# One load of V's weights becomes two, in a fused attention and gated-MLP kernel

## The chip, the cores and the metric

The kernel runs on one core of a Trainium2 chip. The metric is the device time of one execution in microseconds (us). It was measured three times for the kernel before: median 308.36, from 307.97 to 308.63.

## The reference

The input x has 2048 rows of 640 numbers (bf16). The rows are normalized, and two branches of the result are added to x: sliding-window attention with 32 heads of 20 columns and a window of 256 rows, and a gated MLP of width 1536.

```python
xn = _layernorm(x)
q, k, v = split(xn @ wqkv)                  # wqkv is 640 x 1920: Q, K and V columns
p = softmax(where(mask, q @ k.T * 20**-0.5, -1e9))   # causal, 256 back
A = (p @ v) @ wo
B = (sigmoid(xn @ w_gate) * (xn @ w_up)) @ w_down
return x + A + B
```

## The kernel before

The 2048 rows are worked in four chunks of 512, a chunk in four blocks of 128 rows. Every product contracts over 640 numbers, so it takes five matmuls that add into one accumulator, one for each contraction block of 128. For that the normalized rows have to be transposed: `xnT[0][:, d, ...]` holds contraction block d of chunk 0. The order on every engine is that in which the code is written; each engine runs its own list in order and waits on semaphores where it needs the work of another.

The change touches the start, chunk 0. It goes like this.

**Loads.** SP issues the loads one after the other (L183 to L190): the rows of blocks 0, 1 and 3 of x (`load_rows`, L177, 160 KB each), the weights of V's columns 0 to 319 (`load_v(0)`, L181, 400 KB: 128 partitions, five contraction blocks, 320 columns of two bytes), the rows of block 2, V's columns 320 to 639 (`load_v(1)`), and Q's and K's weights (`load_wqkv`, L171, 800 KB each). Later come parts of the gate and up weights (L202) and zeros for two scratch tensors (L199). All go into one queue that 16 DMA engines serve; each engine moves its share of every transfer and reports its end, and a transfer has landed at the sixteenth report. Eight semaphores are handed out to the transfers in turn, so from the ninth on a transfer is issued only when the one eight places before it has landed.

**Normalizing.** For blocks 0 and 3, DVE makes mean and variance (L268, L274) and ACT the root (L654). For blocks 1 and 2, ACT makes the mean (`mean_act`, L664), the sum of squares (L669) and the root (L670). DVE then takes a reciprocal (L658 or L674) and writes the normalized rows `xn` (L292 or L675).

**Transposing.** PE transposes five 128x128 pieces of a block into `pt` (`transpose_rows`, L299), and ACT (block 0, in pieces of three and two) or DVE (the others) copies them to `xnT` (L300).

**V.** `project_v(c, s, hf)` (L364 to L371) multiplies block s with the weights of column half hf: five matmuls over 320 columns (L368) into a PSUM tile of the pool `ps_d`, which has four buffers handed out in turn. `copy_v` (L377) then casts the result into the V tiles, 64 rows per instruction, on DVE or ACT.

These steps are interleaved by hand between L679 and L716. On PE the order is: transposes of block 0; seven warming matmuls; transposes of block 1; V of block 0, first half (v00 in the code); v10; transposes of block 3; v01; v30; v11; transposes of block 2; v31; and both halves of block 2. After that come Q and K of chunk 0 (`g_qk`, L331), then the MLP and attention, with PE at work almost without a break. The first `ps_d` buffer goes to the warming matmuls, the next to v00, v10 and v01; v30 takes the warming buffer again, v11 that of v00, v31 that of v10. A buffer can be written again when its casts are done. The casts of v00 are one on DVE and one on ACT:

```python
    xn2, neg2 = mean_act(2)
    r2 = root_act(2, xn2, neg2)
    norm(3, mv3, r3)
    v10 = project_v(0, 1, 0)
    copy_v(0, 0, 0, v00, dve, (0,))
    transpose_rows(3, dve)
    v01 = project_v(0, 0, 1)
    norm_act(2, xn2, neg2, r2)
    copy_v(0, 0, 0, v00, act, (1,))
```

Of the kernel before, what the change touches and what calls it, by code (L numbers as in the profile page):

```python
# [15 lines left out]
DC = D // P  # L16
# [9 lines left out]
HALF = 320  # L26
# [86 lines left out]
def kernel(  # L113
# [11 lines left out]
    nc = tc.nc  # L125
# [36 lines left out]
    wv = const.tile([P, DC, D], BF16, name="wv")  # L162
    wqkv_r = A_wqkv.rearrange("(c p) n -> p c n", p=P)
# [12 lines left out]
    def load_rows(s, queue):  # L176
        queue.dma_start(out=xc[0][:, s, :], in_=xr[:, s, :])  # L177

    def load_v(hf):
        a = 2 * D + hf * HALF  # L180
        nc.sync.dma_start(out=wv[:, :, hf * HALF:(hf + 1) * HALF], in_=wqkv_r[:, :, a:a + HALF])  # L181

    load_rows(0, nc.sync)  # L183
    load_rows(1, nc.sync)
    load_rows(3, nc.sync)
    load_v(0)
    load_rows(2, nc.sync)
    load_v(1)
    load_wqkv(0)
    load_wqkv(1)  # L190
# [662 lines left out]
```

## Time and profile before

The profiled execution took 308.43 us; its span, from the first to the last instruction, is 306.7.

| | us | share of the span |
|---|---|---|
| PE (matmuls) | 299.9 | 98% |
| ACT | 197.5 | 64% |
| DVE | 179.9 | 59% |
| POOL | 173.0 | 56% |
| 0 to 2 us: PE busy, DMA share | 1.16 | 0.09 |
| 2 to 14 us: PE busy, DMA share | 11.41 of 12.00 | 1.01 |
| 14 us to the end: PE busy, DMA share | 287.30 of 292.70 | 0.36 |

A busy PE includes warming matmuls, which compute nothing of the result; up to 5.3 us PE does nothing else. The DMA share is the mean busy share of the 16 DMA engines. The views used below are the chain of work that ended last (followed back from the last instruction), the timeline of the engines' instructions with the idle time before each and what released it, the sums of a stretch, and the trace's completion events of each transfer. L-numbers are lines of the kernel. The granted clock of PE is 1.00 in every stretch.

### The profile page before, as it was taken

What the parts mean: (1) busy time and instruction counts of PE and PEld (TensorE: products, weight loads), DVE (VectorE), ACT (ScalarE), POOL (GpSimd) and SP (SyncE); (2) the same over time, 40 slices, a digit from 0 to 9 for tenths busy, and PEclk for the clock granted to TensorE, in tenths of its full rate; (3) what the DMA queues carried; (4) which work ended last, traced back from release to release, by engine and by line L of the source; (5) the groups of instructions that cost most, each with busy time, mean ns of one, the idle gap of its engine ahead of it and who ended that gap; (6) DMA issues with size and microseconds to landing.
All of it is one profiled execution on the core that took longest, in us unless ns stands there. A gap on an engine that the chain in (4) does not pass through costs nothing.

```text
span 306.7 us, 10106 instructions
## 1 busy us (share of the span) xinstructions
PE 299.9 (98%) x4341; PEld 168.0 (55%) x4376; DVE 179.9 (59%) x356; ACT 197.5 (64%) x194; POOL 173.0 (56%) x314
## 2 busy tenths in 40 slices
PE   8999999999999999999999999999999999999996
PEld 6654444445657654554557654554546664444774
DVE  5735657889866569683826555482733527362433
ACT  6833768688965648888655538979585557778000
POOL 3086667479873728676572827657372756557000
DMA  7998959646574152773001222650000210000202
GB/s 209 364 316 253 320 185 260 206 129 194 141 231 111 44 161 83 235 221 75 4 0 47 65 70 80 193 177 2 2 2 2 66 45 25 0 4 0 88 24 64
DMA packets 40148, 36.04 MB, mean 118 GB/s; under 512 B 9000, under 2 KB 39848, under 8 KB 40104
## 3 DMA queue, kind: packets, MB, share of 16 engines
q1 hardware_dynamic: 39240, 34.63, 37.1%
q10 hardware_dynamic: 864, 0.77, 0.8%
q8 instruction: 34, 0.56, 0.8%
q14 instruction: 10, 0.08, 0.1%
HBM read 24.77 MB, written 10.62 MB: 115 GB/s over the span
## 4 chain that ended last, share of the span: by engine, by line
PE 96%; DMA 2%; issue 1%; SPq 0%; DVE 0%
PE y L481 18%; PE pu L467 17%; PE pg L460 17%; PE pqk L331 14%; PE ps L536 9%; PE pv L368 8%; PE y L488 7%; PE acc L567 6%; DMA wv<-in_A_wqkv_dram 2%; SPq L177 0%; PE pt L299 0%; DVE xn L492 0%
## 5 line engine op out<-in xcount | busy, mean ns | idle before, releaser
L548 POOL TENSOR_SCALAR_AFFINE_SELECT pT<-pT 64x512 bf16<-64x512 bf16 (+1 forms) x252 | 152.4, 605 | 90.7 <-ACT pT L541 79.0
L541 ACT ACTIVATE pT<-ps 128x2048 bf16<-128x2048 f32 x75 | 140.8, 1877 | 58.8 <-PE ps L536 57.8
L471 DVE SCALAR_TENSOR_TENSOR h<-th,pu 128x512 bf16<-128x512 f32 x48 | 32.7, 683 | 55.9 <-PE pu L467 42.7
L467 PE MATMUL pu<-xnT,wu 128*128 128x512 bf16 x230 | 58.9, 380 | 0.7 <-issue 0.3
L460 PE MATMUL pg<-xnT,wg 128*128 128x512 bf16 x225 | 58.3, 380 | 1.2 <-issue 0.6
L481 PE MATMUL y<-wd,h 128*128 128x320 bf16 (+2 forms) x396 | 56.6, 295 | 0.0
L331 PE MATMUL pqk<-xnT,wqk 128*128 128x512 bf16 x190 | 44.9, 380 | 0.7 <-issue 0.3
L481 PEld LDWEIGHTS <-h 128*128 128x128 bf16 x396 | 36.7, 98 | 15.9 <-issue 2.2
L463 ACT ACTIVATE th<-pg 128x512 f32<-128x512 f32 x48 | 28.6, 596 | 15.3 <-PE pg L460 15.1
L460 PEld LDWEIGHTS <-wg 128*128 128x128 bf16 x240 | 22.2, 98 | 25.7 <-issue 2.0
L467 PEld LDWEIGHTS <-wu 128*128 128x128 bf16 x240 | 22.1, 98 | 25.4 <-issue 1.8
L536 PE MATMUL ps<-qT,kT 20*64 20x320 bf16 (+4 forms) x1456 | 31.9, 259 | 0.0
L331 PEld LDWEIGHTS <-wqk 128*128 128x128 bf16 x200 | 19.5, 103 | 21.2 <-issue 1.2
L579 DVE STREAM_TRANSPOSE t<-acc 128x512 f32<-128x512 f32 x32 | 21.1, 695 | 13.7 <-PE acc L567 13.7
L536 PEld LDWEIGHTS <-kT 20*64 20x64 bf16 x1456 | 15.7, 103 | 24.5 <-issue 22.0
L492 DVE SCALAR_TENSOR_TENSOR rows<-y,rows 128x320 bf16<-128x320 f32 x30 | 14.3, 484 | 21.4 <-PE y L488 21.1
L368 PE MATMUL pv<-wv,xnT 128*128 128x320 bf16 x160 | 25.8, 300 | 0.3 <-DMA wv<-in_A_wqkv_dram 0.3
L488 PE MATMUL y<-wo,oc 128*128 128x320 bf16 (+2 forms) x165 | 24.2, 295 | 0.0
L567 PE MATMUL acc<-pT,v 64*32 64x320 bf16 (+4 forms) x1456 | 19.7, 252 | 0.0
L567 PEld LDWEIGHTS <-v 64*32 64x32 bf16 x1456 | 16.4, 91 | 5.9 <-ACT pT L541 1.3
L368 PEld LDWEIGHTS <-xnT 128*128 128x128 bf16 x160 | 14.6, 98 | 8.9 <-issue 1.6
L591 DVE TENSOR_TENSOR on<-t,rec 128x320 bf16<-128x320 f32 (+1 forms) x32 | 18.6, 580 | 1.1
(52 smaller groups left out, 187.8 us busy)
## 6 DMA issues: line engine op xcount, KB each, us to landing
qT<-sq SPq DMA_DIRECT2D x16, 256.0 KB
kT<-sk SPq DMA_DIRECT2D x16, 256.0 KB
sq<-st SPq DMA_DIRECT2D x20, 128.0 KB
sk<-st SPq DMA_DIRECT2D x20, 128.0 KB
out_dram<-rows SPq DMA_DIRECT2D x15, 160.0 KB
wg<-in_B_w_gate_dram SPq DMA_DIRECT2D x4, 480.0 KB
wu<-in_B_w_up_dram SPq DMA_DIRECT2D x4, 480.0 KB
xc<-in_A_x_dram SPq DMA_DIRECT2D x3, 640.0 KB
```

Of the source, the lines that this page charges most:

```text
L331: nc.tensor.matmul(ps, lhsT=wt[:, m, :], rhs=xnT[c][:, d, :], start=(d == 0), stop=(d == DC - 1))
L368: nc.tensor.matmul(ps[:, 0:HALF], lhsT=xnT[c][:, d, s * P:(s + 1) * P], rhs=wv[:, d, hf * HALF:(hf + 1) * HALF], start=(d == 0), stop=(d = ...
L460: nc.tensor.matmul(pg, lhsT=part(wg, d, f), rhs=xnT[c][:, d, :], start=(d == 0), stop=(d == DC - 1))
L463: nc.scalar.activation(out=th, in_=pg, func=TANH, scale=0.5)
L467: nc.tensor.matmul(pu, lhsT=part(wu, d, f), rhs=xnT[c][:, d, :], start=(d == 0), stop=(d == DC - 1))
L471: nc.vector.scalar_tensor_tensor(out=h, in0=th, scalar=1.0, in1=pu, op0=ADD, op1=MULT)
L481: nc.tensor.matmul(y[:, 0:cut[1] - cut[0]], lhsT=ht[c, f][:, s * P:(s + 1) * P], rhs=wd[:, f, cut[0]:cut[1]], start=(f == 0), stop=False)
L488: nc.tensor.matmul(y[:, 0:cut[1] - cut[0]], lhsT=oc[c, m][:, s * P:(s + 1) * P], rhs=wo[:, m, cut[0]:cut[1]], start=False, stop=(m == DC - 1))
L536: nc.tensor.matmul(ps[a * U:(a + 1) * U, i, col * U:(col + n) * U], lhsT=qk["k", kc, o // GH][32 * i:32 * i + DH, o % GH + a, kb * U:(kb + ...
L541: nc.scalar.activation(out=pt[:, :, 0:CW], in_=ps, func=EXP, scale=SCALE)
L548: nc.gpsimd.affine_select(out=view, in_=view, pattern=[[0, HG], [0, n], [sign, U]], compare_op=GE, fill=0.0, base=base, channel_multiplier ...
L567: nc.tensor.matmul(acc[32 * i:32 * i + 32, q * U:(q + n) * U], lhsT=vt[kb][a * U:(a + 1) * U, u, h * VW:h * VW + 32], rhs=pt[a * U:(a + 1) ...
```

## The change

`load_v` gets a range of contraction blocks, and the first column half is loaded by two transfers in a row: blocks 0 to 2 (240 KB) and blocks 3 to 4 (160 KB). Every other load keeps its place behind them, and the second column half stays one transfer.

```diff
-    def load_v(hf):
+    def load_v(hf, lo=0, hi=DC):
         a = 2 * D + hf * HALF
-        nc.sync.dma_start(out=wv[:, :, hf * HALF:(hf + 1) * HALF], in_=wqkv_r[:, :, a:a + HALF])
+        nc.sync.dma_start(out=wv[:, lo:hi, hf * HALF:(hf + 1) * HALF], in_=wqkv_r[:, lo:hi, a:a + HALF])
 
     load_rows(0, nc.sync)
     load_rows(1, nc.sync)
     load_rows(3, nc.sync)
-    load_v(0)
+    load_v(0, 0, 3)
+    load_v(0, 3, DC)
     load_rows(2, nc.sync)
     load_v(1)
     load_wqkv(0)
```

In the instruction lists, SP has one transfer more, and the fourth matmul of v00 waits for the second of the two. K's weights become the ninth transfer, which waits for the landing of block 0's rows. All other instructions, their order and what they wait for are the same; after the first transfers the semaphores are handed out one place further on.

## The prediction

> **What bounds the kernel now.** I read the page first, then the chain of work that ended last from 0 to 34 us, then the timeline of each engine from 6 to 14 us, and last the sums of that stretch.
>
> ```profile
> PE 299.9 (98%) x4341; PEld 168.0 (55%) x4376; DVE 179.9 (59%) x356; ACT 197.5 (64%) x194; POOL 173.0 (56%) x314
> ```
>
> PE is busy 98% of the 306.7 us span, and the later chain is almost all PE. So whatever the start gains or loses is carried to the end one for one, and nothing else is in play. The chain in the start (start us, us, what):
>
> ```profile
> 2.19 4.92 DMA wv<-in_A_wqkv_dram
> 7.11 0.04 issue
> 7.15 1.52 PE pv L368 x10
> 8.67 0.28 PE pt L299 x5
> 8.95 2.12 PE pv L368 x15
> 11.06 0.28 PE pt L299 x5
> 11.34 2.15 PE pv L368 x15
> ```
>
> It says that the first half of V's weights lands at 7.11 and that PE runs from there. Taken alone, this promises the whole wait to the change. But the chain names one releaser per step and hides those that came a few hundredths earlier. They are in the timeline (start, us, engine, line, idle before):
>
> ```profile
> 6.68 0.10 PEld L368 LDWEIGHTS <-xnT 128*128 128x128 bf16 x1
> ...
> 7.15 1.52 PE L368 MATMUL pv<-wv,xnT 128*128 128x320 bf16 x10 [0.25 <-DMA wv<-in_A_wqkv_dram]
> ...
> 7.56 0.74 ACT L664 ACTIVATE xn<-xc 128x640 bf16<-128x640 bf16 x1 [0.20 <-DMA xc<-in_A_x_dram]
> ...
> 9.70 2.19 ACT L377 CAST v<-pv 64x320 bf16<-64x320 f32 x5
> 9.70 0.16 DVE L674 RECIPROCAL rstd<-rstd 128x1 f32<-128x1 f32 x1 [0.23 <-ACT rstd L670]
> 9.90 0.45 DVE L675 TENSOR_SCALAR xn<-xc,neg,rstd 128x640 bf16<-128x640 bf16 x1
> 10.38 1.00 DVE L377 CAST v<-pv 64x320 bf16<-64x320 f32 x2
> ...
> 11.41 0.49 DVE L300 COPY xnT<-pt 128x640 bf16<-128x640 bf16 x1
> ...
> 11.95 1.20 PEld L368 LDWEIGHTS <-xnT 128*128 128x128 bf16 x10 [0.27 <-DVE xnT L300]
> ```
>
> The second chain to see: rows of block 2 (xc) land just before 7.56. From there ACT (mean, squares, root; its rows at 8.42 and 9.38 are among those left out), then DVE (reciprocal, normalize, two casts of v01, copy of the transpose) run without a free moment up to 11.90, and PE's last two V products start on that copy at 11.95.
>
> **The change, step by step.** I write vst for the product of row block s with column half t; PE's order is v00, v10, transposes of block 3, v01, v30, v11, transposes of block 2, v31, v20, v21. A V matmul starts every 0.135 us ((1.52-0.30)/9, 0.30 being the length of one), so a product of five takes 0.68; a transpose takes 0.056 (0.28/5).
>
> *Removed: the wait for blocks 3 and 4.* The weights' load for v00 starts at 6.68; a later product starts its first matmul 0.05 after its load (8.73 and 8.78), so v00 could start at 6.73. It starts at 7.15: 0.42 us wait. The second part is 128x2x640 = 163,840 bytes, at the 328 GB/s of 4.6 to 6.8 us 0.50 us of transfer. So my estimate for the first part is 7.11-0.50 = 6.61, ahead of the 6.69 that no wait needs. Bounds: 7.11 (all of the wait stays) and 6.73 or earlier (all goes).
>
> *Added: a wait on v00's fourth matmul* for blocks 3 and 4. Queued behind it on PE is everything else. It comes at 6.73+3x0.135 = 7.14; the data at about 7.11. Cost 0.00 to 0.04, and the next step covers it.
>
> *What is late next.* v10 needs xnT of block 1: DVE copies it 6.95 to 7.43, so 7.49 instead of 7.82 (0.33 left). Transposes of block 3 after it: 8.17 (their input is ready at 8.04). v01 could start at 8.45, but needs the second column half, whose last completion event in the trace is at 8.64: 8.68 instead of 8.78 (0.10 left). v30 starts when v01's matmuls are through, 9.36, instead of 9.53. v11 writes the accumulator of v00, which ACT reads in the first of the casts from 9.70, 0.42 each: 10.12, plus 0.05 to PE, 10.17 instead of 10.22 (0.05 left). v20 needs the copy of block 2 at 11.41 to 11.90: 11.95, as now. **0.00 left.** From v20 to the Q projection at 13.32 PE is dense, and it stays so.
>
> So the wait of 0.42 is cut into pieces and stands again ahead of v10, v01, v11 and v20. The start is worth what block 2's landing moves, and nothing else.
>
> *Moved: block 2's rows, V's second half and Q's and K's weights are issued one SP instruction later*, 0.48 us (2.19 to 2.67). In the queue this does not show if the 16 engines are behind anyway. DMA share 1.01 and 1.07 from 4.6 us on (sums of the stretches, next-to-last column) and this row of SP say they are:
>
> ```profile
> 3.71 2.26 SPq L171 DMA_DIRECT2D wqk<-in_A_wqkv_dram  x2
> ```
>
> An issue takes 0.43 to 0.53 when free; two take 2.26 here, because SP is held up by a full queue. Block 2 is issued at 2.67 and used at 7.56; block 0 is issued at 0.80 and used at 3.11. Thus some 2.6 us of the 4.89 are queueing, and 0.48 hides in them. The cost of a further transfer in the queue itself is not to be seen in before alone. From above, 0.48 (the issue pitch, as if nothing hid it). From below, -0.59: PE's idle places from 6.73 to 13.32 sum to 0.42+0.07+0.10, and block 2 can't give more than PE can take. Block 2's 163,840 bytes follow the half of wv within 0.45 (7.11 to 7.56), which at 363 GB/s are their own transfer time: a boundary between transfers costs nothing there. That is the nearest row, and I take 0.00. Q's weights are used 13.19 and K's near 18.7 (13.32+25x0.216, the first 25 matmuls of Q and K at five to 1.08); the completion events have them at 10.91 and 13.20, so 0.48 is covered there.
>
> *Waits on eight-back transfers.* Each transfer from the ninth on waits for the one eight before it; one more transfer makes K's weights the ninth, waiting for block 0 (used 3.11, issue after 4.28): 0. All other waits keep their partners from there on, and compute instructions and their order are the same but for the one wait.
>
> Sum: 308.43 (the profiled execution: 306.7 span and 1.73 around it; the median is 308.36, the runs 307.97 to 308.63) + 0.00 = **308.4**.
>
> The Trainium skill speaks for splitting under a condition: "Perfetto Trace Analysis", section DMA Optimizations, says that smaller pieces may start sooner if the DMA engines are generally idle. The shares above say that this condition is not met, and by that rule the sum would be the same.
>
> **The rivals.**
>
> *A. Slower: block 2 lands later.* The DMA share dips to 0.73 (151 GB/s) from 3.4 to 4.6, when the engines turn from x to V's weights, and the sixteenth completion of that transfer comes at 7.11, the fifteenth at 6.41. One engine pays 0.70 for its start. If the second transfer makes it pay again, block 2, v20 and the end come 0.70 later: 309.1; with only the issue slip, 308.9. It decides as soon as the landing comes after 7.56, for there is no slack behind. For it: the dip. Against it: no such lag is added at block 2 or wv's second half, which follow in a full queue.
>
> *B. Faster: the dip fills.* Smaller pieces let engines that now wait start sooner, and block 2 lands earlier. Half of what PE can take, 0.3, gives 308.1; the limit 0.59 gives 307.8. For: the same dip. Against: bytes and packets are the same, and the late engine has its first packets in the first part either way.
>
> *C. It does not do what it says:* the late engine holds back the first part too, to 7.1. PE waits as now: 308.4. The fifteen others landed by 6.41, so all hangs on that engine.
>
> *D. A fixed price per transfer, in series.* A lone transfer takes 2.31 (0.80 to 3.11) from issue to use; if block 2 had to wait for that once more: 310.7. Against: the 0.45 above. The Trainium skill, "DMA: Bandwidth & Descriptors", section Anatomy of one DMA, gives about 2.0 us fixed per transfer (for those issued by GpSimd); by that 310.4; the trace's 0.45 between two landings speaks against paying it in series.
>
> **How the numbers follow.** 0.2% is 0.62 us, about what a measurement of this kernel can tell from no change. Forecast 0.50, C 0.12, B 0.13, A 0.22, D 0.03. Forecast and C stay within 0.62 but for the runs' own scatter of about 0.3 (0.02 faster, 0.04 slower). B reaches 0.62 only at its limit with scatter: 0.08 of 0.13 faster. A passes it at 0.70: 0.16 of 0.22 slower; D all. So faster 0.10, same 0.67, slower 0.23. The range: from B's limit less a little scatter, 307.7, to A's 309.1 with a little, 309.2.
>
> **What would show it.** After: v00 starts near 6.73; PE's idle time for wv is gone or 0.04; ACT's first pass over block 2 still starts at 7.5 to 7.6; v20's load waits longer for DVE's copy (0.27 now); the Q projection starts at 13.3. If it starts earlier, block 2 landed earlier (B); later with a late ACT pass, A. I am wrong in the working if the Q projection moves while ACT's pass does not, or if the end moves while the Q projection doesn't.

## The result and the profile after

The changed kernel takes 309.2 us (median of 11 runs, 308.61 to 309.68); the kernel before took 308.36 beside it (11 runs, 307.97 to 308.83). The ratio is 1.0026, with a 95% interval of 1.0018 to 1.0034: slower by 0.8 us. The profiled execution of after took 309.34, with a span of 307.5 (308.43 and 306.7 before).

The page of after:

```profile
span 307.5 us, 10107 instructions
...
PE 300.0 (98%) x4341; PEld 168.3 (55%) x4376; DVE 180.2 (59%) x356; ACT 197.4 (64%) x194; POOL 172.8 (56%) x314
```

PE's busy time grew by 0.1, the span by 0.8. So PE does the same work and stands idle longer. From the first matmul of the Q projection to the last of PE, the traces have 290.61 before and 290.49 after. All of the loss is ahead of the Q projection, which starts at 14.12 instead of 13.32. The chain of work that ended last, in the start (start us, us, what):

```profile
3.70 5.94 DMA wv<-in_A_wqkv_dram
9.64 0.04 issue
9.69 2.20 PE pv L369 x15
11.88 0.28 PE pt L300 x5
12.16 2.12 PE pv L369 x15
14.28 0.22 PE pqk L332
```

Before, the weights in the chain were those issued at 2.19, V's first half. Now they are those issued at 3.70: **V's second half**, a transfer that the change does not touch. The timeline shows where PE stands (start, us, engine, line, idle before):

```profile
6.78 1.60 PE L369 MATMUL pv<-wv,xnT 128*128 128x320 bf16 x10
...
7.31 0.72 ACT L665 ACTIVATE xn<-xc 128x640 bf16<-128x640 bf16 x1
...
7.52 0.52 PEld L369 LDWEIGHTS <-xnT 128*128 128x128 bf16 x5 [0.24 <-DVE xnT L301]
...
9.69 2.20 PE L369 MATMUL pv<-wv,xnT 128*128 128x320 bf16 x15 [1.03 <-DMA wv<-in_A_wqkv_dram]
...
12.75 1.20 PEld L369 LDWEIGHTS <-xnT 128*128 128x128 bf16 x10 [0.24 <-DVE xnT L301]
```

v00 starts at 6.78 instead of 7.15, v10's load waits for the copy of block 1 at 7.52, and ACT's pass over block 2 starts at 7.31 instead of 7.56. All this is early or as forecast. Then v01 stands 1.03 us for the second column half, which landed at 9.64 (8.64 before). (The listed idle counts from the modelled end of the matmul before it. By start times the wait is 1.19: in before v01 follows the first transpose of block 3 after 0.28, here after 1.47.) v00 started 0.37 earlier than before, v01 starts 0.91 later (9.69 against 8.78).

SP's rows of after (start, us):

```profile
2.18 0.96 SPq L181 DMA_DIRECT2D wv<-in_A_wqkv_dram  x2
3.19 0.47 SPq L177 DMA_DIRECT2D xc<-in_A_x_dram  x1
3.70 0.43 SPq L181 DMA_DIRECT2D wv<-in_A_wqkv_dram  x1
```

V's second half is issued at 3.70 instead of 3.23 and lands 1.00 later: the 0.47 of its place, and 0.53 more. The sums from 6 to 8 us (the last two columns are the DMA share and GB/s), of before and then of after:

```profile
6.00:8.00 2.00, 1.47 (x15) 0.96 (x13) 1.93 (x6) 1.17 (x4) 0.00 (x0) 1.00 1.06 349
```

```profile
6.00:8.00 2.00, 2.00 (x22) 1.48 (x21) 1.93 (x7) 1.54 (x5) 0.00 (x0) 1.00 0.83 214
```

The queue that the forecast took for full did not stay so in after. In the stretch in which block 2 ends and V's second half begins, its engines moved 214 GB/s instead of 349.

### The profile page after: what moved, and what is told of

The parts are those of the page before. It is cut to its first block, busy times and chain, and to the rows that moved or that the text cites. A ratio compares the mean times of both kernels' runs of the same rounds, so it can differ in the third digit from the quotient of the medians.

```text
span 307.5 us, 10107 instructions
## 1 busy us (share of the span) xinstructions
PE 300.0 (98%) x4341; PEld 168.3 (55%) x4376; DVE 180.2 (59%) x356; ACT 197.4 (64%) x194; POOL 172.8 (56%) x314
## 4 chain that ended last, share of the span: by engine, by line
PE 95%; DMA 2%; issue 1%; SPq 1%; DVE 0%
PE y L482 18%; PE pu L468 17%; PE pg L461 17%; PE pqk L332 14%; PE ps L537 9%; PE y L489 7%; PE pv L369 7%; PE acc L568 6%; DMA wv<-in_A_wqkv_dram 2%; SPq L177 1%; SPq L181 0%; DVE xn L493 0%; PE pt L300 0%
```

## The experiments

Two theories. **The place**: a further transfer ahead of V's second half makes SP issue that half 0.48 later, and its landing follows its issue; that the further transfer is a split does not matter. **The split** (the rival): the pieces themselves, their boundary or their smaller size, cost time in the engines. In the expectations theory 1 is the place, theory 2 the split, and theory 3 an accident of one execution. Ratios are against the kernel before on the same chip, with 95% intervals.

### Both kernels once more

No edit.

> The changed kernel once more, for a second trace. In its first trace V's second column half landed at 9.64 us (8.64 before) and PE waited 1.03 us for it, while block 2 landed at 7.06 (7.54 before). Theory 1 (issue slip: whatever stands one place later in SP's list comes later) and theory 2 (thin queue: with the smaller pieces the engines reach V's second half with little queued, and pay for its start again) both expect the wait again, 0.7 to 1.1 us, and a ratio near 1.0026. Theory 3 (accident of one execution, with the loss elsewhere) expects a wait that is far from 1.0, 0 to 0.4.

> The kernel before once more, one look. Theories 1 and 2 expect V's second half at 8.5 to 8.8 us and no wait of PE for it, with the wait for the first half (0.3 to 0.5) and block 2 near 7.5. Theory 3 expects one of the two to move by half a us or more.

After again: 308.93 (10 runs), ratio 1.0018 (1.0006 to 1.0031). Its profiled execution shows the same wait in the same place; V's second half, issued at 3.69, landed at 9.82:

```profile
9.86 2.20 PE L369 MATMUL pv<-wv,xnT 128*128 128x320 bf16 x15 [1.03 <-DMA wv<-in_A_wqkv_dram]
```

Before again, one run, 308.28 with a span of 306.5:

```profile
6.79 1.60 PE L368 MATMUL pv<-wv,xnT 128*128 128x320 bf16 x10
...
8.50 2.28 PE L368 MATMUL pv<-wv,xnT 128*128 128x320 bf16 x15
```

Here V's first half landed at 6.61 and v00 waited for no weights. The wait of 0.42 that the forecast set out to remove belongs to one execution of before. Of the seven traces with this half unsplit in its old place (before twice and five experiments), none of the other six has it. In one of them it is hidden by chance: with the small transfer behind V's second half the first half landed at 6.97, and v00's weights were loaded only at 6.94, since PE's earlier work came late.

The expectation for before again was missed: 8.5 to 8.8 for V's second half and the old wait. It landed at 8.13, about half a us earlier, which had been given as a sign of theory 3. The landings do scatter that much; the ratios of after in two sets of runs, 1.0026 and 1.0018, say that the loss is no accident.

### A small transfer in place of the split

```diff
     load_v(0)
+    dum = const.tile([P, 32], BF16, name="dum")
+    nc.sync.dma_start(out=dum, in_=xr[:, 2, 0:32])
     load_rows(2, nc.sync)
```

The 8 KB are not used. It was run twice, the second time on another chip.

> The kernel before with the first half of V's weights in one transfer, and a small extra transfer (128 rows of 64 bytes of x into a tile nobody reads) behind it, where the second part stands in the changed kernel. Block 2 and V's second half are so issued one place later, without the split. Theory 1: V's second half lands near 9.6, PE waits for it 0.7 to 1.0, ratio 1.002 to 1.003. Theory 2: the first half holds the engines up as before, the second half lands at 8.6 to 8.8, ratio 1.000 to 1.0006. Theory 3: ratio 1.000.

> The small extra transfer instead of the split again (the kernel before with 128 rows of 64 bytes loaded where the second part stands), in more rounds, since its first interval held both theories. Theory 1 (the later issue alone makes V's second half late): ratio 1.0018 to 1.003, and a wait of PE for V's second half of 0.7 or more. Theory 2 (the split itself, by the thinner queue, makes it late): ratio 0.9995 to 1.0008 and a wait of 0 to 0.3. A ratio between, 1.0008 to 1.0018, with a wait near the 0.36 of its first trace: each gives a part.

308.55, ratio 1.0011 (0.9994 to 1.0028, 10 runs), and 308.84, ratio 1.0019 (1.0009 to 1.0029, 11 runs). In the first trace V's second half was issued at 3.70, landed at 9.02, and PE waited; ratio and wait lie between the two theories:

```profile
9.06 2.20 PE L370 MATMUL pv<-wv,xnT 128*128 128x320 bf16 x15 [0.36 <-DMA wv<-in_A_wqkv_dram]
```

In the second trace the same half, issued at 3.69, landed at 8.61:

```profile
8.65 2.20 PE L370 MATMUL pv<-wv,xnT 128*128 128x320 bf16 x15
```

No idle time is listed, and by start times the wait is 0.19 (8.65, 0.47 after the first transpose of block 3, instead of 0.28). So the ratio is the one that theory 1 expected, the wait the one that theory 2 expected. That execution took 308.22, near the lower end of its runs: five of them lie from 308.17 to 308.49, six from 308.84 to 309.48. So a small transfer with no split costs, within the intervals, what the change costs, but not the same in each execution. One trace alone would have misled here.

### The second half ahead of block 2

After, with the two loads exchanged, so that V's second half gets its old issue time back and block 2 pays for it.

```diff
-    load_rows(2, nc.sync)
     load_v(1)
+    load_rows(2, nc.sync)
```

> The changed kernel with V's second half issued ahead of block 2, so that it is issued when it was before (near 3.2 us), and block 2 a place after it. Theory 1: V's second half lands at 8.2 to 8.7 and PE waits for it 0 to 0.2; block 2 lands at 7.5 to 8.2, and what it is late after 7.56 stands ahead of v11 or v20: ratio 1.000 to 1.002. Theory 2: V's second half still starts in a thin queue, lands at 9.0 to 9.4 and PE waits 0.4 to 0.8; ratio 1.002 to 1.004.

309.93, ratio 1.0041 (1.0023 to 1.0059, 5 runs). V's second half, issued at 3.19, landed at 7.92 and v01 did not wait for it. Block 2, issued at 3.70, landed at 8.40 (7.06 in after). ACT's pass over it started 0.99 after ACT was free, ACT's casts came later, and v11, which writes a buffer that ACT has to read first, stood for them:

```profile
8.43 0.74 ACT L665 ACTIVATE xn<-xc 128x640 bf16<-128x640 bf16 x1 [0.99 <-DMA xc<-in_A_x_dram]
```

```profile
11.04 0.84 PE L369 MATMUL pv<-wv,xnT 128*128 128x320 bf16 x5 [0.91 <-ACT v L378]
```

The ratio lies above both ranges (1.000 to 1.002 for theory 1, 1.002 to 1.004 for theory 2), and the landing at 7.92 is earlier than both. V's second half has its old issue time here, but the 160 KB of block 2 now come behind it and not ahead, so its early landing does not test the place alone. And block 2 has the 400 KB of V ahead of it: it landed 0.48 after them, about the 0.43 that it took behind the first half in before (7.11 to 7.54). Its lateness goes with its turn in the queue and can't be put down to the slot. That block 2 has little room was right.

### The split without the later place: part of the loads on ACT's queue

Three kernels take one early load off SP's list and give it to ACT, which I expected to issue it at about 2.3, behind its table load. `scr` is the tile of ACT's first small instruction, moved ahead and fed from the constants, so that it waits for nobody.

```diff
+    nc.scalar.activation(out=scr, in_=ones[:, 0:1], func=SQRT)
     load_v(0, 0, 3)
-    load_v(0, 3, DC)
+    load_v(0, 3, DC, nc.scalar)
...
-    nc.scalar.activation(out=scr, in_=eps, func=SQRT)
```

`load_v` gets the queue as a further argument. The second kernel is before with `load_rows(2, nc.scalar)` and no split; the third is after with `load_rows(2, nc.scalar)`; both have `scr` moved in the same way.

> The split without the later issue: blocks 0 to 2 from SP as in the changed kernel, blocks 3 to 4 from ACT's queue at about 2.3 us, where ACT has nothing to do (the activation that loads ACT's table reads a constant instead of eps, so that it need not wait). SP's list is then as before, block 2 at 2.7 and V's second half at 3.2. Theory 1: V's second half lands at 8.1 to 8.7, PE waits 0 to 0.2 for it; ratio 0.999 to 1.0005. Theory 2: it lands at 9.2 or later, PE waits 0.5 to 1.0; ratio 1.0015 to 1.003.

> No split; block 2's rows are issued from ACT's queue at about 2.3 us, so that V's second half moves one place up in SP's list (2.7 instead of 3.2). Theory 1: its landing follows its issue, 7.7 to 8.2, no wait; block 2 lands earlier than 7.0, so PE's waits ahead of v20 shrink; ratio 0.998 to 0.9995 if the first half is not much later than 6.7. Theory 2 says the same of block 2 and expects V's second half no earlier than 8.1; ratio 0.9985 to 1.0.

> The split as in the changed kernel, both parts from SP, with block 2's rows from ACT's queue at about 2.3 us: V's second half is issued at 3.2, as before the change. Theory 1: lands at 8.1 to 8.7, PE's wait for it 0 to 0.2, ratio 0.998 to 1.0003. Theory 2: lands at 9 or later, PE waits 0.4 to 0.9, ratio 1.001 to 1.003.

Ratios 1.0013 (1.0004 to 1.0021, 11 runs), 1.0016 (1.0007 to 1.0026, 12 runs) and 1.0013 (1.0004 to 1.0022, 11 runs). The intended issue time was missed. ACT issued at 0.86, beside its table load, and its transfer ran among the rows of x. Block 1 landed at 4.09 instead of 3.5, and ACT's first pass, the head of the chain to v00, came late. ACT's queue and first pass in the first of the three:

```profile
0.86 0.45 ACTq L181 DMA_DIRECT2D wv<-in_A_wqkv_dram  x1
...
4.11 0.74 ACT L665 ACTIVATE xn<-xc 128x640 bf16<-128x640 bf16 x1 [1.82 <-DMA xc<-in_A_x_dram]
```

PE of the same kernel:

```profile
7.29 1.60 PE L369 MATMUL pv<-wv,xnT 128*128 128x320 bf16 x10
...
9.01 2.28 PE L369 MATMUL pv<-wv,xnT 128*128 128x320 bf16 x15
```

v00 starts at 7.29 and v01 at 9.01 without a wait for weights. That is a price of its own, about 0.5, and it hides the total. All three ratios lie above the ranges of theory 1 (the first in neither range, the second above both, the third in theory 2's), but with this price in them they decide nothing between the theories. The landing can be read all the same: with the split kept and V's second half issued at 3.18 and 3.19, it landed at 7.81 and 7.93 (first and third kernel). In these two traces the boundary within the first half does not delay it. The second kernel, issued at 2.66, landed it at 8.85, which the place alone does not explain. The Trainium skill ("Perfetto Trace Analysis", section DMA Optimizations) suggests spreading DMAs over the engines that can issue them where issuing is the limit; these three ratios do not bear it out here, since the second queue delayed the rows.

### The second part on ACT's queue, issued later

The same with ACT's first instruction left in its old place (it ends at 3.0) and the load behind it.

```diff
     nc.scalar.activation(out=scr, in_=eps, func=SQRT)
+    load_v(0, 3, DC, nc.scalar)
```

> After, but the second part (blocks 3 and 4) goes through ACT's queue, issued after ACT's one early instruction (the row that waits for eps until 2.80), so at about 3.0. SP's list is then that of before: block 2 at 2.67, V's second half at 3.2. Theory of the place (V's second half is late because SP issues it one place later): second half lands at 8.7 or earlier, PE waits under 0.1 ahead of v01, v00 starts near 6.8, Q projection 13.0 to 13.35, ratio 0.998 to 1.0005. Theory of the split (one more transfer of weights costs wherever it is issued): second half lands after 9, PE waits 0.4 or more ahead of v01, Q projection 13.7 or later, ratio 1.0015 or more. A transfer in a queue of its own may also delay block 2; that would show as ACT's first pass over block 2 after 7.6.

309.94, ratio 1.0062 (1.0044 to 1.008, 6 runs): a miss of both theories. ACT issued at 3.57, not at 3.0: as the tenth transfer in turn, it was handed the semaphore of block 1's rows and waited for their landing, at 3.55. By then ACT's first pass was due, and behind the issue it moved from 3.54 to 4.11. The part landed at 8.38, and PE stood within v00:

```profile
3.57 0.49 ACTq L181 DMA_DIRECT2D wv<-in_A_wqkv_dram  x1
```

```profile
7.29 0.57 PE L369 MATMUL pv<-wv,xnT 128*128 128x320 bf16 x3
...
8.42 1.11 PE L369 MATMUL pv<-wv,xnT 128*128 128x320 bf16 x7 [0.56 <-DMA wv<-in_A_wqkv_dram]
```

It shows what the added wait on v00's fourth matmul costs when its cover is gone. It does not separate the theories, since V's second half (issued at 3.19, landed at 8.71) shared the engines with this part.

### The small transfer behind, and two of them ahead

```diff
     load_v(1)
+    dum = const.tile([P, 32], BF16, name="dum")
+    nc.sync.dma_start(out=dum, in_=xr[:, 2, 0:32])
     load_wqkv(0)
```

> Before with one small transfer (32 columns of block 2's rows, 8 KB, not used) behind V's second half instead of ahead of block 2. Q's and K's weights go one place later, V's second half keeps its place at 3.2. Theory of the place: second half lands as in before (8.1 to 8.7), no new wait, ratio 0.999 to 1.0005. Theory of the further transfer (any one more transfer in these queues costs): ratio 1.0015 or more, as with the small transfer ahead of block 2 (1.0019).

308.38, ratio 1.0007 (0.9997 to 1.0016, 12 runs). V's second half was issued at 3.21, landed at 8.51, and v01 did not wait:

```profile
8.71 2.28 PE L370 MATMUL pv<-wv,xnT 128*128 128x320 bf16 x15
```

By the trace the place decides. By the time alone it is open: 1.0007 lies between the two expectations, a little above that of the place, and its interval overlaps that of the small transfer ahead (1.0009 to 1.0029).

The second kernel has two such transfers (columns 0 to 31 and 32 to 63) behind `load_v(0)`, so V's second half comes two places later.

> Before with two small transfers (8 KB each, not used) ahead of block 2: the suspected cost twice. V's second half is issued at about 4.2 instead of 3.22, block 2 at about 3.7. Theory of the place: second half lands at 9 to 10 and PE waits 0.4 to 1.4 ahead of v01, with less scatter than with one place; ratio 1.002 to 1.005, more than the 1.0019 of one. If the cost does not grow with the places (1.001 to 1.002 again), the place is not the cause.

309.23, ratio 1.0029 (1.0015 to 1.0044, 8 runs). V's second half, issued at 4.17, landed at 9.72:

```profile
6.71 1.60 PE L371 MATMUL pv<-wv,xnT 128*128 128x320 bf16 x10
...
9.76 2.20 PE L371 MATMUL pv<-wv,xnT 128*128 128x320 bf16 x15 [1.17 <-DMA wv<-in_A_wqkv_dram]
```

Ratio, landing and wait are as the place expected. The smaller scatter is not: the runs lie from 308.52 to 310.11.

### The first half in three transfers

```diff
-    load_v(0, 0, 3)
-    load_v(0, 3, DC)
+    load_v(0, 0, 2)
+    load_v(0, 2, 4)
+    load_v(0, 4, DC)
```

> After with the first half in three transfers (blocks 0 to 1, 2 to 3, 4): two places more than before, and two boundaries. Theory of the place: as the run with two small transfers, within 0.001 of its ratio, V's second half issued at about 4.2. Theory of the split: more than the two small transfers by 0.001 or over, since the boundaries between pieces of weights cost by themselves.

309.51, ratio 1.0032 (1.0018 to 1.0046, 9 runs). V's second half was issued at 4.15 and landed at 9.44:

```profile
6.84 1.60 PE L370 MATMUL pv<-wv,xnT 128*128 128x320 bf16 x10
...
9.48 2.20 PE L370 MATMUL pv<-wv,xnT 128*128 128x320 bf16 x15 [0.76 <-DMA wv<-in_A_wqkv_dram]
```

It is within 0.001 of the run with two small transfers, as the place has it. The intervals are too wide to exclude a further 0.001 from the boundaries.

### What the runs say together

Of the kernels whose loads all go through SP in before's order, with V's second half put off by 0, 1 or 2 places (issue and landing in one trace each):

| | places | issued | landed | listed wait ahead of v01 | ratio |
|---|---|---|---|---|---|
| before | 0 | 3.23 | 8.64 | 0 | 1 |
| before again | 0 | 3.22 | 8.13 | 0 | one run |
| small transfer behind | 0 | 3.21 | 8.51 | 0 | 1.0007 |
| after | 1 | 3.70 | 9.64 | 1.03 | 1.0026 |
| after again | 1 | 3.69 | 9.82 | 1.03 | 1.0018 |
| small transfer | 1 | 3.70 | 9.02 | 0.36 | 1.0011 |
| small transfer, second run | 1 | 3.69 | 8.61 | 0 (0.19 by start times) | 1.0019 |
| two small transfers | 2 | 4.17 | 9.72 | 1.17 | 1.0029 |
| three parts | 2 | 4.15 | 9.44 | 0.76 | 1.0032 |

The mean ratio of one place is 1.0019, which is 0.57 us of 308.3; of two places 1.0031, 0.94 us. That is about one issue pitch (0.48) for each place. The intervals of one and two places overlap pair by pair, but over all runs the mean time stands 0.59 us above that of before with one place (42 runs) and 1.05 us with two (17 runs). Kernels with a split and without stand mixed. From issue to landing it takes 5.21 on average with 0 places, 5.58 with one, 5.42 with two, with single values from 4.91 to 6.13. So on average the landing of V's second half follows its issue; the bytes ahead of it, which but for the 8 or 16 KB of the small transfers are the same in all of them, do not fix it. The engines' rate from 6 to 8 us says the same: 325 to 354 GB/s in the three traces with 0 places, 214 to 309 in the six with one or two. The DMA share does not say it: in three parts it is 1.08 at 265 GB/s. What the intervals leave open is a part that belongs to the split alone: 0.0022 for the two runs of after against 0.0015 for those of the small transfer, about 0.2 us, is within their scatter. And every run that puts V's second half off does it by one more transfer ahead on SP. No run delays the issue alone, so a price of a further transfer in SP's queue, however small, is not separated from the place.

No kernel here beats before.

## The prediction step by step: where it was right and where it was wrong

The time, 309.2, is the upper end of the range given. That end was the price of rival A, a late block 2, with a little scatter. Block 2 was not late, so that the range holds the time is luck. The forecast of no measurable change was wrong: the loss, 0.26%, is beyond 0.2%.

- *What bounds the kernel*: right. The Q projection moved by 0.80, the span by 0.8.
- *Removed, the wait for blocks 3 and 4*: right in after's trace. The two parts landed at 5.77 and 6.33, and v00 started at 6.78 (forecast 6.73). But the wait was read from one execution; before again had none. There was less to gain than 0.42, however the rest went. And with both parts in by 6.33, ahead of the load of v00's weights at 6.72, after's trace doesn't show that it was the split that took the wait away.
- *Added, the wait on v00's fourth matmul*: 0.00, as forecast. The run with ACT's late issue shows 0.56 when the data come at 8.38.
- *Late next, v10*: right, its load waits for block 1's copy and starts at 7.52 (forecast 7.49).
- *Late next, v01: "8.68 instead of 8.78 (0.10 left)"*: wrong. It started at 9.69. The step took the landing of V's second half from before, 8.64, as if it stood still, although the next part lists this very transfer as one that is issued later.
- ***Moved, "0.48 hides in them … I take 0.00"*: this is the step that failed.** The true cost is near the bound it gave from above, 0.48 for the place (0.57 on average over four comparisons, 0.8 in after's own). The argument compared a lone transfer's time from issue to use with block 2's and called the difference queueing. Block 2 did bear it out: it landed at 7.06, earlier than before's 7.54, though issued 0.52 later. V's second half, the next transfer, did not: issued 0.47 later, it landed 1.00 later. The row of 2.26 that was to show a full queue is of transfers behind V's second half, whose own issue, 0.43, was as short as when free; so it could not show that this transfer's place is hidden.
- *"0.00 left" at v20; block 2 alone decides*: wrong. Block 2 came 0.48 earlier and nothing followed, because v01 came late. Having looked for the tightest wait (0.00 at v20), I did not ask which of the tight ones the moved transfers feed; 0.10 at v01 is as good as none against 0.48. The sign given for this step did not come either: v20's load waits 0.24 for DVE's copy, not longer than 0.27.
- *Moved, Q's and K's weights; the waits eight back*: right, PE does not wait for Q's or K's weights in any trace.
- *Rival A* had the direction, and its 308.9 for the issue slip alone is the price nearest to the cause (309.1, nearer in number, was for a further 0.70 of one engine ahead of block 2, which no trace shows). Its place was wrong: block 2 was not late, and ACT's pass did not move back. The text's own test says so: the Q projection moved while ACT's pass did not.
- *Rivals B, C and D*: block 2 did land earlier than in before's trace, as B has it, but before again has it at 7.03 without the change, and the end gained nothing by it; the first part did land early, so C did not occur; nothing paid a serial 2.31.

The Trainium skill's rule ("Perfetto Trace Analysis", section DMA Optimizations: splitting may let some pieces start sooner, and where the DMA engines are generally idle the whole may end sooner) came out half and half. The first piece did land sooner, at 5.77; the sum came out later, and what was lost was lost by a transfer behind the pieces, of which that rule says nothing.

**Why the landing loses more than the place** is read from the traces afterwards, and no run tested it by itself. Call "lead" the time from a transfer's issue to the first engine's completion of the transfer ahead, and "own time" the mean over the engines from one completion to the next. For V's second half the own time is 1.13 to 1.17 where the lead is 2.37 or more (before 2.75, before again 2.52, small transfer behind 2.83, and the first and third kernel with ACT's queue, 2.37 and 2.43). It is 1.40 to 1.91 where the lead is 2.29 or less (after 2.28, after again 2.15, small transfer 2.12 and 2.29, two small transfers 1.83, three parts 2.07, the exchange 1.85, the late ACT issue 2.03). The first engine came free of block 2 at 5.98 in before and in after alike. So a slip of 0.47 took the lead from 2.75 to 2.28, and the own time went from 1.17 to 1.91. In the exchange the lead is short at the old issue time, because its turn came earlier; that is nearer to theory 2, which has the engines reach V's second half with little queued, than to the place. One kernel does not fit: block 2 alone on ACT's queue has a lead of 2.81 and an own time of 1.58. Why a transfer that has been issued some two microseconds ahead of its turn still runs slower stays open, and so does why the same kernel lands it at 9.02 in one execution and at 8.61 in another.

## What to carry to other kernels

A transfer added to one queue puts off the issue of every transfer behind it by a slot (here 0.48 us). Here one landing followed on average (V's second half) and one did not (block 2: 6.75 to 7.23 with one place, 7.03 to 7.54 with none). So the question is not only what the split transfer gains but which later transfer is used with the least room. A nearly full DMA share did not show that a later issue is hidden; put the issue times and landings of all transfers of the stretch side by side and reckon with a landing that follows its issue, unless a run shows the contrary. A wait of 0.4 us in one profiled execution may not be there in the next, so a second profile of the same kernel comes ahead of any plan to remove it.

## What the runs showed of the hardware that was not expected

- The landing of one and the same transfer varies by up to 0.5 us between executions of a kernel: V's second half at 8.64 and 8.13 (before), 9.02 and 8.61 (small transfer).
- A transfer lands with the slowest of the 16 engines. In after, V's second half was reported by the first engine at 7.31, the eighth at 8.24, the fifteenth at 9.27 and the sixteenth at 9.64; in after again the sixteenth came 1.47 behind the fifteenth (9.82 and 8.35).
- ACT can issue a transfer while its table load runs (issued at 0.86, table load from 0.80 to 2.08).
